# Single PSUM banks in the first token half of an MLP, its down pieces on two alternating pairs

## The chip, the cores and the metric

One core of one Trainium2 chip runs the kernel. The metric is the time of one execution in device microseconds. The kernel before takes 2958.96 us, the median of three runs (2958.73 to 2962.72). The profile is of one further execution.

The engines are named as the profile does: PE is TensorE (PEld its weight loads), DVE is VectorE, ACT is ScalarE, POOL is GpSimd, SP is SyncE, which here only issues DMAs. Each engine works through its instructions in the order in which the program issues them.

## The reference

```python
x = A_x                                            # [1, 2048, 576] float32
mod = (silu(c) @ w_mod).reshape(1, 6, 1, 576)
sa, ca, ga, sb, cb, gb = ...                       # six rows of 576
h = layernorm(x) * (1 + ca) + sa
q = h @ wq                                         # 32 heads of 128
k, v = the last 512 positions of the caches        # 16 heads, each for two q heads
o = softmax(q @ k^T * 128 ** -0.5) @ v
x = x + ga * (o @ wo)
h = layernorm(x) * (1 + cb) + sb
gate = h @ W_gate                                  # [2048, 4608]
up = h @ W_up
x = x + gb * ((relu(gate) * up) @ W_down)          # [4608, 576]
```

Everything is float32. The kernel keeps that precision by splitting an operand into a rounded part (hi) and the rest (lo): a product is three matmuls, hi by hi, hi by lo and lo by hi.

## The kernel before, in words

The program runs the attention first (128 units, one q head by 512 queries each) and the MLP after it. The 2048 rows of x lie in sixteen tiles acc0 to acc15 of 128 tokens by 576; attention and MLP both add their results into them.

**The MLP's passes.** The MLP works on one half of the tokens after the other (1024 tokens each). W_gate and W_up have 36 column tiles of 128 (NFT); a pass m takes two of them. NFP = 18 passes make a half, so m = 0 to 17 are the first half and m = 18 to 35 the second (NB = 36). The gate and up product of a pass is a 2 x 2 block product: two column tiles, two halves of the 576 inputs, two blocks of 512 tokens. It is done with seven products instead of eight (the scheme of Strassen and Winograd): P1, P6, P2, P7, P5, P4, P3, in this order (order). Each is a slot of the pass. A slot has two halves (prod), the gate's (xx = 0) and the up's (xx = 1), with seven matmuls of 512 columns each into one PSUM bank. P2 is accumulated onto P1's banks and P3 onto P5's, after those have been read.

**The extra operands.** The sums of weights that P6, P7, P5 and P3 need are made by VectorE from SBUF (w_sums, line 851: S1 in slot 1, S4 in slot 2, S3 and S2 of the next pass in slots 5 and 6) in the first half only. w_prep, two slots ahead of the product, splits them: ScalarE rounds (line 821) and GpSimd subtracts (lines 822 and 823). The split weights are also stored to DRAM, and the second half only loads them. From m = 5 on, the first half also prepares the second half's activations (h_later, lines 883 to 899, mostly GpSimd). Four times (m = 2, 4, 6, 8) half a block of second-half tokens is normalized (ln_half): VectorE's statistics, ScalarE's scaling, ten transposes by TensorE into PSUM in two steps (trans, line 1027), copies by ScalarE (line 1030) and stores to DRAM on SP's queue.

**After a product.** VectorE and ScalarE take the product out of PSUM (evac in the first half, evac_half in the second), combine it with the earlier ones, and form relu(gate) * up; ScalarE and GpSimd split the result (h_out, lines 1060 and 1061).

**The down product.** In the first half pass m - 1's down product runs in the slots of pass m, in eight pieces (md_piece, down_piece): a piece has twelve matmuls of 288 columns into a PSUM pair (two banks) and an addition into acc by VectorE (line 602). One piece lies between the two halves of every slot but the first, and one more stands at the end of slots 0 and 1. In the second half most passes (FAST, m = 18 to 33) do the down product with a scheme of seven products as well, in fourteen smaller pieces of six matmuls (fast_piece, line 671), run in the following pass. That scheme needs extra sums beside the result; they lie in acc0 to acc7, whose tokens are done. The first pass of it (FAST[0] = 18) writes them, by a copy on ScalarE (line 679); the later ones add (line 681).

**PSUM.** There are eight banks. In the first half of the MLP, three pairs rotate for gate and up: two of the pool psS (tag s) and one of psX (tag x); new_banks takes the next free one, and a pair goes back to the list free after its evacuation. The fourth pair, psW (tag w), takes every down piece. The transposes of ln_half take a pair of the rotation. In the second half psS is closed, and its four banks become psG: two tags, a and b, of two single banks each, so that the gate's bank and the up's bank are waited for apart; P1, P2, P5, P3 of an even pass use a and P6, P7, P4 use b, and the other way round in an odd one. Pair x is then free for the down pieces, which alternate between x and w (md_pool) from m = 19 on.

**Order of issue.** mlp_slots writes the order by hand. For a slot: the first half of the product, then sums and others (weight sums, splits, loads), then in the second half evac_half of the first bank, then a down piece with its addition, then the functions set by mat with sums=True, then the second half of the product, then the evacuation. The function mat(m, s, fn) places fn in slot s + 1 of pass m; with s = 5 it is P3's slot.

Of the kernel before, what the change touches and what calls it, by code (L numbers as in the profile page):

```python
# [7 lines left out]
F32 = mybir.dt.float32  # L8
# [6 lines left out]
P = 128  # L15
# [10 lines left out]
H2 = D // 2  # L26
# [5 lines left out]
def kernel(  # L32
# [13 lines left out]
    nc = tc.nc  # L46
# [594 lines left out]

    NFP = NFT // 2
    NB = 2 * NFP
    ds_, hhi, hlo = {}, {}, {}
    wop, wraw, hop = {}, {}, {}
    pair, tmp = {}, {}
# [13 lines left out]
    def fast_piece(m, kind, n):  # L660
        if kind == "4":
            specs = [(fop[m, "A22"], fw[m, "4"], 0, 2 * n + j) for j in range(2)]
        else:
            a, b = {"16": ("A11", "S2"), "75": ("S3", "S1"), "23": ("A12", "S4")}[kind]
            specs = [(fop[m, x], fw[m, kind], j * H2, n) for j, x in enumerate((a, b))]
        pool = md_pool()
        ps = pool[0].tile([P, 2, 512], F32, tag=pool[1], name=f"mf{m}_{kind}_{n}")
        for j, ((hi, lo), (whi, wlo), c, qt) in enumerate(specs):
            sl = slice(qt * P, (qt + 1) * P)
            for i, (x, w) in enumerate(((hi, whi), (hi, wlo), (lo, whi))):  # L670
                nc.tensor.matmul(ps[:, j, :H2], x[:, sl], w[:, c:c + H2], start=i == 0, stop=i == 2)  # L671
        if kind == "4":
            for j in range(2):
                a = acc[8 + 2 * n + j][:, :H2]
                nc.vector.tensor_tensor(a, ps[:, j, :H2], a, op=ALU.add)
            return
        a = acc[{"16": 0, "75": 4, "23": 12}[kind] + n].rearrange("p (h n) -> p h n", h=2)
        if kind != "23" and m == FAST[0]:
            nc.scalar.copy(a, ps[:, :, :H2])
        else:  # L680
            nc.vector.tensor_tensor(a, ps[:, :, :H2], a, op=ALU.add)

# [304 lines left out]
    def ln_half(qb, hh):  # L987

        ts = [4 * qb + 2 * hh, 4 * qb + 2 * hh + 1]
        st, xn = {}, []  # L990
        nm = f"lh{qb}_{hh}"
        cols = slice(256 * hh, 256 * hh + 256)

        def stats():
            mv = st["mv"] = sp.tile([P, 4, 2], F32, tag="mv", name=f"mv{nm}")
            for i, t in enumerate(ts):
                assert adds[t] == HQ // 2
                bn = sp.tile([P, 2, 6], F32, tag="st", name=f"st{nm}_{i}", bufs=1)
                for h in range(2):
                    nc.vector.bn_stats(bn[:, h, :], acc[t][:, h * H2:(h + 1) * H2])  # L1000
                nc.vector.bn_aggr(mv[:, i, :], bn)
            rs = st["rs"] = sp.tile([P, 2, 4], F32, tag="rs", name=f"rs{nm}")
            nc.gpsimd.tensor_scalar(rs[:, 0, :2], mv[:, :2, 1], EPS, None, op0=ALU.add)
            nc.gpsimd.tensor_tensor(rs[:, 0, :2], rs[:, 0, :2], mhalf[:, :2], op=ALU.pow)
            nc.gpsimd.tensor_tensor(rs[:, 1, :2], mv[:, :2, 0], rs[:, 0, :2], op=ALU.mult)
            nc.gpsimd.tensor_scalar(rs[:, 1, :2], rs[:, 1, :2], -1.0, None, op0=ALU.mult)

        def norm():
            for i, t in enumerate(ts):
                pool, tag = ((rp, "raw"), (xp, "xm"))[i]  # L1010
                n = pool.tile([P, 640], F32, tag=tag, name=f"xn{nm}_{i}")
                nc.scalar.activation(n[:, :D], acc[t], AF.Identity, bias=st["rs"][:, 1, i:i + 1],
                                     scale=st["rs"][:, 0, i:i + 1])
                xn.append(n)

        def trans(ds):
            ps, k = new_banks(f"lt{nm}_{ds[0]}")
            free.append(k)
            ps = ps.rearrange("p a (b n) -> p (a b) n", b=2)
            p = 64 if ds[0] == 4 else P  # L1020
            if ds[0] == 4:
                f = hp.tile([P, 512], F32, tag="hT", name=f"lf{nm}_4").rearrange("p (a n) -> p a n", a=2)
            else:
                f = wp.tile([P, 4, 256], F32, tag="wC", name=f"lf{nm}_0")
            for j, d in enumerate(ds):
                for i in range(2):
                    nc.tensor.transpose(ps[:p, j, i * P:(i + 1) * P], xn[i][:, d * P:d * P + p], ident)
            add, mul = mods["b"]
            for j, d in enumerate(ds):
                nc.scalar.activation(f[:p, j, :], ps[:p, j, :], AF.Identity, bias=add[:p, d:d + 1],  # L1030
                                     scale=mul[:p, d:d + 1])
                hb_store(qb, d, cols, f[:p, j, :])

        return [stats, norm, lambda: trans((4,)), lambda: trans((0, 1, 2, 3))]

    def prod(m, s, n, xx):

        hs, w = hop[m // NFP, OPS[s][1]], wop[n]
        ps = pair[m, s][:, xx, :] if m < NFP else pair[m, s][xx]
        ops = []  # L1040
        for t in range(2):
            ops += [(w[:, xx, t, :], hs[t]), (w[:, xx, 3 + t, :], hs[t]), (w[:, xx, t, :], hs[3 + t])]
        ops.append((w[0:96, xx, 2, :], hs[2][0:96]))
        for i, (a, c) in enumerate(ops):
            nc.tensor.matmul(ps, a, c, start=s not in ("P2", "P3") and i == 0, stop=i == len(ops) - 1,  # L1045
                             skip_group_check=True)
# [101 lines left out]
    def md_pool():  # L1148
        px["n"] = px.get("n", 0) + 1
        return (px["x"], "x") if px["n"] % 2 else (psW, "w")  # L1150

    def new_banks(nm):
        npair[0] += 1
        k = free.pop(0)
        return (px["x"] if k == "x" else psS).tile([P, 2, 512], F32, tag=k, name=nm), k

    def new_pair(m, s):
        if m < NFP:
            pair[m, s], kind[m, s] = new_banks(f"gu{npair[0]}")
            return  # L1160
        if "g" not in px:
            open_g()
        kind[m, s] = "ab"[(s in ("P6", "P7", "P4")) ^ m % 2]
        pair[m, s] = [px["g"].tile([P, 512], F32, tag=kind[m, s], name=f"gh{m}_{s}_{i}") for i in range(2)]
# [220 lines left out]
    def mat(m, s, fn, sums=False):  # L1385
        mextra.setdefault((m, s, sums) if s < 6 else (m + 1, -1, sums), []).append(fn)

    for m in range(NB):
# [3 lines left out]
        for f in range(2):  # L1392
            for k, fn in enumerate(wd_prep(m, f)):
                if m >= NFP:
                    at_ = m, 3 + f
# [5 lines left out]
    fast_end()  # L1401
    for i in range(4):
        m = 2 + 2 * i
        for at_, fn in zip(((m - 1, 5), (m, 2), (m, 3), (m, 4)), ln_half(2 + i // 2, i % 2)):
            mat(*at_, fn, sums=at_ == (m - 1, 5))
    later = {s: [fn for t in range(3) for fn in h_later(1, s, t)] for s in TERMS}
    for i, fn in enumerate(later.pop("B11") + later.pop("B21")):
        mat(5 + i // 3, (0, 2, 4)[i % 3], fn)
# [18 lines left out]

    def mlp_slots():
        for m in range(NB):
            md = [lambda k=k, qt=qt: md_piece(m - 1, k, qt, md_pool() if m > NFP else None)  # L1430
                  for k in range(2) for qt in range(4)] if m else []
            if m - 1 in FAST:
                md = fast_pieces(m - 1)
            for i, s in enumerate(order(m)):
                flush_stores()
                if s not in ("P2", "P3"):
                    new_pair(m, s)
                else:
                    pair[m, s], kind[m, s] = (x[m, {"P2": "P1", "P3": "P5"}[s]] for x in (pair, kind))
                prod(m, s, 7 * m + i, 0)  # L1440
                if m or i:
                    sums(m, i)
                    others(m, i)
                if m >= NFP:
                    evac_half(m, s, 0)
                if m and i or m - 1 in FAST:
                    md.pop(0)()
                elif filler and not m:
                    filler.pop(0)()
                for fn in mextra.pop((m, i - 1, True), []):  # L1450
                    fn()
                prod(m, s, 7 * m + i, 1)
                wop.pop(7 * m + i)
                if m >= NFP:
                    evac_half(m, s, 1)
                if m and i < 2 or m - 1 in FAST:
                    md.pop(0)()
                elif filler and not i:
                    filler.pop(0)()
                if m < NFP:  # L1460
                    evac(m, s)
                if s not in ("P1", "P5") and m < NFP:
                    free.append(kind[m, s])
                yield
        for k in range(2):
            for qt in range(4):
                md_piece(NB - 1, k, qt, md_pool())
        flush_stores()
        assert not mextra and not filler
# [203 lines left out]
```

## Time and profile before

| | before |
|---|---|
| median of three runs | 2958.96 us |
| the profiled execution | 2957.22 us |
| its span | 2955.4 us |
| TensorE busy | 2871.7 us, 97% |
| VectorE busy | 2184.3 us, 74% |
| ScalarE busy | 1434.2 us, 49% |
| GpSimd busy | 2196.4 us, 74% |
| mean granted clock of TensorE | 0.991 |
| first token half of the MLP | about 1652 to 2322 us |

The times of the trace count from the start of the span. In the list of waits a row names who waited and for whom, then microseconds in total, times, and the longest. In the chain of waits a row is a start, a duration and a piece of work; x12 is one down piece, x7 one half of a product. In the timeline a bracket at the end of a row is the idle time before it and who ended it. A row by stretches has its length and then each engine's busy time with the number of instructions, the granted clock, the DMA engines' share and GB/s.

### The profile page before, as it was taken

The numbers are of one execution on the slowest core, as the hardware profiler recorded it, in microseconds if no ns is written. First come the engines' busy times: TensorE is split into PE (matmuls) and PEld (weight loads), VectorE is DVE, ScalarE is ACT, GpSimd is POOL, SyncE is SP. The second block draws the span as 40 slices with busy tenths as digits, with TensorE's granted clock in tenths as the row PEclk, the third lists the DMA queues.
The fourth block names the chain that finished last, engine by engine and source line by source line (L and its number), as shares of the span: only waits on it lengthen the run. The fifth ranks groups of instructions, "written<-read, shape, count | busy, mean of one in ns | idle before, by whom it ended". The sixth has DMA issues, their size and how long they took to land.

```text
span 2955.4 us, 41574 instructions
## 1 busy us (share of the span) xinstructions
PE 2871.7 (97%) x15256; PEld 2496.5 (84%) x15256; DVE 2184.3 (74%) x3058; ACT 1434.2 (49%) x2015; POOL 2196.4 (74%) x1597
## 2 busy tenths in 40 slices
PE   6889999999999999999999999999999999999999
PEld 5678888888888888888888788888888888888888
DVE  5778888788788888777889677777777556666665
ACT  3656666666676666666656433333323132222220
POOL 3767888788888889877778666667777477777773
PEclk8999999999999999999999999999999999999999
DMA  5312222222223223322144355566667944444443
GB/s 182 118 68 87 85 86 83 70 100 85 94 84 112 84 69 122 110 69 85 65 144 139 111 195 206 211 224 237 240 225 247 328 142 150 161 156 150 151 150 136
DMA packets 165899, 410.61 MB, mean 139 GB/s; under 512 B 15040, under 2 KB 61888, under 8 KB 165696
## 3 DMA queue, kind: packets, MB, share of 16 engines
q1 hardware_dynamic: 132944, 289.23, 30.3%
q10 hardware_dynamic: 32752, 118.73, 10.1%
q8 instruction: 121, 1.98, 0.3%
q14 instruction: 82, 0.67, 0.1%
HBM read 275.81 MB, written 160.40 MB: 148 GB/s over the span
## 4 chain that ended last, share of the span: by engine, by line
PE 85%; DVE 6%; POOL 3%; ACT 2%; DMA 2%; issue 2%; SPq 0%; ACTq 0%; DVEq 0%; POOLq 0%
PE gh_P L1045 13%; PE wo L591 13%; PE qps L388 12%; PE gu L1045 11%; PE md L591 8%; PE mf L671 6%; PE s L464 3%; PE s L463 3%; PE s L462 3%; PE pv L566 3%; PE pv L565 3%; PE pv L564 3%; DVE wr L851 2%; POOL lo L546 1%; PE qm L490 1%
## 5 line engine op out<-in xcount | busy, mean ns | idle before, releaser
L546 POOL TENSOR_TENSOR lo<-p,hi 128x1024 fp32r<-128x1024 f32 x256 | 611.7, 2411 | 0.0
L555 POOL TENSOR_TENSOR ks<-ks,p 128x512 f32<-128x512 f32 x256 | 344.1, 1344 | 284.1 <-ACT p L539 213.5
L467 DVE TRANSPOSE_TENSOR_REDUCE t<-s 128x32 f32<-128x1024 f32 x256 | 316.3, 1243 | 136.5 <-PE s L464 125.5
L537 DVE TENSOR_TENSOR p<-s,mb 128x1024 f32<-128x1024 f32 x250 | 295.2, 1219 | 4.2
L388 PE MATMUL qps<-hTa,wA 128*128 128x512 f32 x1176 | 285.4, 393 | 4.4 <-ACT wA L186 2.0
L591 PE MATMUL wo<-woga,ohi 128*128 128x288 f32 x1344 | 279.9, 301 | 0.0
L591 PE MATMUL md<-wogb,hhi 128*128 128x288 f32 x1280 | 263.1, 298 | 14.6 <-DVE acc L602 14.6
L539 ACT ACTIVATE p<-p 128x1024 f32<-128x1024 f32 x250 | 264.1, 1056 | 17.6 <-DVE p L537 15.7
L526 ACT CAST hi<-p 128x1024 fp32r<-128x1024 f32 x256 | 269.0, 1051 | 7.0
L388 PEld LDWEIGHTS qps<-hTa,wA 128*128 128x128 f32 x1176 | 223.0, 190 | 53.3 <-ACT wA L186 2.7
L1045 PE MATMUL gh_P<-hop_T,wop 128*128 128x512 f32 (+1 forms) x1008 | 255.8, 393 | 1.3 <-DMA wop<-wk_P 1.3
L442 ACT ACTIVATE qhi<-qps 128x512 fp32r<-128x512 f32 x128 | 76.5, 597 | 341.6 <-PE qps L388 341.6
L591 PEld LDWEIGHTS md<-wogb,hhi 128*128 128x128 f32 x1280 | 214.2, 189 | 29.5 <-DVE acc L602 18.6
L602 DVE TENSOR_TENSOR acc<-md,acc 128x576 f32<-128x576 f32 x160 | 120.8, 755 | 147.8 <-PE md L591 146.9
L591 PEld LDWEIGHTS wo<-woga,ohi 128*128 128x128 f32 x1344 | 218.4, 189 | 6.6
L1045 PEld LDWEIGHTS gh_P<-hop_T,wop 128*128 128x128 f32 (+1 forms) x1008 | 181.4, 188 | 33.2 <-DMA wop<-wk_P 1.7
L591 PE MATMUL wo<-woga,olo 128*128 128x288 f32 x672 | 198.5, 295 | 0.4 <-POOL olo L580 0.2
L1045 PE MATMUL gh_P<-hop_B,wop 128*128 128x512 f32 (+1 forms) x756 | 192.7, 395 | 0.0
L591 PE MATMUL md<-wogb,hlo 128*128 128x288 f32 x640 | 189.9, 297 | 0.0
L1045 PE MATMUL gu<-hop_B,wop 128*128 128x512 f32 (+1 forms) x756 | 187.4, 394 | 0.0
L600 ACT COPY acc<-wo 128x576 f32<-128x576 f32 x232 | 147.7, 636 | 69.2 <-PE wo L591 61.7
L580 POOL TENSOR_TENSOR olo<-rb,ohi 128x512 fp32r<-128x512 f32 x128 | 167.1, 1305 | 16.8 <-ACT ohi L576 16.5
(275 smaller groups left out, 7651.3 us busy)
## 6 DMA issues: line engine op xcount, KB each, us to landing
wop<-wk_P SPq DMA_DIRECT2D x133, 640.0 KB
wk_P<-wop ACTq DMA_DIRECT2D x119, 640.0 KB
wr<-wlay SPq DMA_DIRECT2D x68, 384.0 KB
againq<-akq SPq DMA_DIRECT2D x22, 640.0 KB
againo<-ako SPq DMA_DIRECT2D x18, 576.0 KB
rogb<-wd SPq DMA_DIRECT2D x36, 288.0 KB
rwA<-wq SPq DMA_DIRECT2D x32, 320.0 KB
wlay<-wg SPq DMA_DIRECT2D x36, 256.0 KB
```

Of the source, the lines that this page charges most:

```text
L388: return [lambda i=i, a=a, b=b: nc.tensor.matmul(ps, a, b, start=(i == 0), stop=(i == n - 1)) for i, (a, b) in enumerate(ops)]
L467: nc.vector.tensor_reduce(t4[u][:, 2 * h:2 * h + 2, :].rearrange("p k b -> p (k b)"), t.rearrange("p k (b j) -> p (k b) j", j=32), axis=AX ...
L526: nc.scalar.copy(hi_[u, h], pt[u, h])
L537: nc.vector.tensor_tensor(p, t, bc[u][:, None, :].to_broadcast([P, 2, 512]), op=ALU.subtract)
L539: nc.scalar.activation(p, p, AF.Exp, bias=0.0, scale=1.0)
L546: nc.gpsimd.tensor_sub(lo_[u, h], pt[u, h], hi_[u, h].bitcast(F32))
L555: nc.gpsimd.tensor_tensor(ks_[u], ks_[u], p[:, j, :], op=ALU.add)
L580: nc.gpsimd.tensor_sub(olo[u], o.pop(u), ohi[u].bitcast(F32))
L591: nc.tensor.matmul(ps[:, half, :H2], a[:, sl], w[b][:, cs], start=(n == 0 and seed is None), stop=(n == 5), skip_group_check=seed is not None)
L600: nc.scalar.copy(av, ps[:, :, :H2])
L671: nc.tensor.matmul(ps[:, j, :H2], x[:, sl], w[:, c:c + H2], start=i == 0, stop=i == 2)
L1045: nc.tensor.matmul(ps, a, c, start=s not in ("P2", "P3") and i == 0, stop=i == len(ops) - 1, skip_group_check=True)
```

## The change

A constant NG = 1 takes the place of NFP wherever the choice between pairs and single banks is made. So only pass 0 still rotates three pairs; from m = 1 on gate and up use the single banks of psG and evac_half. All down pieces of m = 1 on alternate between x and w. The transposes of ln_half take a turn in that alternation, and the step with four blocks moves from slot 5 of its pass, ahead of the down piece, to slot 6, behind it. The first extra sums of the second half are copied by VectorE instead of ScalarE.

```diff
+    NG = 1
...
         if kind != "23" and m == FAST[0]:
-            nc.scalar.copy(a, ps[:, :, :H2])
+            nc.vector.tensor_copy(a, ps[:, :, :H2])
...
         def trans(ds):
-            ps, k = new_banks(f"lt{nm}_{ds[0]}")
-            free.append(k)
+            pool = md_pool()
+            ps = pool[0].tile([P, 2, 512], F32, tag=pool[1], name=f"lt{nm}_{ds[0]}")
...
-        ps = pair[m, s][:, xx, :] if m < NFP else pair[m, s][xx]
+        ps = pair[m, s][:, xx, :] if m < NG else pair[m, s][xx]
...
     def new_pair(m, s):
-        if m < NFP:
+        if m < NG:
...
-        for at_, fn in zip(((m - 1, 5), (m, 2), (m, 3), (m, 4)), ln_half(2 + i // 2, i % 2)):
-            mat(*at_, fn, sums=at_ == (m - 1, 5))
+        for at_, fn in zip(((m - 1, 5), (m, 2), (m, 3), (m, 5)), ln_half(2 + i // 2, i % 2)):
+            mat(*at_, fn, sums=at_[1] == 5)
...
-            md = [lambda k=k, qt=qt: md_piece(m - 1, k, qt, md_pool() if m > NFP else None)
+            md = [lambda k=k, qt=qt: md_piece(m - 1, k, qt, md_pool())
...
-                if m >= NFP:
+                if m >= NG:
                     evac_half(m, s, 0)
...
-                if m >= NFP:
+                if m >= NG:
                     evac_half(m, s, 1)
...
-                if m < NFP:
+                if m < NG:
                     evac(m, s)
-                if s not in ("P1", "P5") and m < NFP:
+                if s not in ("P1", "P5") and m < NG:
                     free.append(kind[m, s])
```

## The prediction

> **What bounds the kernel now.** I read the page's first lines, then the list of waits of TensorE from 1640 us on, then busy time per loop pass in the MLP's first token half, then the chain of waits inside it.
>
> ```profile
> span 2955.4 us, 41574 instructions
> PE 2871.7 (97%) x15256; PEld 2496.5 (84%) x15256; DVE 2184.3 (74%) x3058; ACT 1434.2 (49%) x2015; POOL 2196.4 (74%) x1597
> ```
>
> ```profile
> PE md L591 <- DVE acc L602: 14.6, 9, 3.6
> PE mf L671 <- ACT acc L679: 2.3, 1, 2.3
> PE gh_P L1045 <- DMA wop<-wk_P: 1.3, 1, 1.3
> ```
>
> TensorE is the bound; only what it idles, or does slowly, can be won. The largest wait is that of a down piece (md) for VectorE's add of the piece before it, since all of them use one PSUM pair (w). The passes m = 1 to 16, cut at the start of P3's up half (time, PE, PEld, DVE, ACT, POOL, granted clock, DMA share, GB/s):
>
> ```profile
> 1693.29:1728.57 35.28, 35.28 (x195) 31.23 (x195) 24.83 (x28) 10.93 (x17) 22.13 (x21) 1.00 0.57 202
> 1728.57:1764.99 36.42, 36.42 (x205) 32.18 (x205) 28.77 (x33) 14.60 (x23) 23.51 (x25) 1.00 0.56 199
> ...
> 2021.66:2059.31 37.65, 35.55 (x196) 31.14 (x195) 28.05 (x28) 12.09 (x17) 30.93 (x26) 1.00 0.64 230
> 2059.31:2094.63 35.32, 35.32 (x196) 31.14 (x195) 25.37 (x28) 12.03 (x17) 28.23 (x24) 1.00 0.71 257
> ...
> sum 590.19, PE 575.54 PEld 505.29 DVE 434.75 ACT 200.40 POOL 422.91; mean PE 44.27 PEld 38.87 DVE 33.44 ACT 15.42 POOL 32.53
> ```
>
> An undisturbed pass takes 35.28 us, one with a norm half (m = 2, 4, 6, 8) 36.42. Sixteen of them would be 16 x 35.28 + 4 x 1.14 = 569.0; they took 590.2. Of the 21.2 above that, 590.19 - 575.54 = 14.6 are idle; the rest is work at a lower clock. The chain shows where:
>
> ```profile
> 2130.66 3.11 PE md L591 x12
> 2133.77 5.12 PE gu L1045 x21
> ...
> 2169.43 1.86 PE md L591 x12
> 2171.29 4.83 PE gu L1045 x21
> 2176.12 1.60 PE md L591 x12
> ...
> 2196.95 1.62 PE gu L1045 x7
> ...
> 2200.65 7.22 DVE wr L851
> ...
> 2208.59 2.63 PE md L591 x12
> 2211.23 5.62 PE gu L1045 x21
> ```
>
> ```profile
> 2130.66 0.71 PE L591 MATMUL md<-wogb,hhi 128*128 128x288 f32 x2 [2.35 <-DVE acc L602]
> ```
>
> A piece that follows a stall costs 1.85 to 3.11 instead of 1.60: 1.51 + 0.29 at 2130, 1.03 + 0.79 at 2208, 0.25 at each of the other seven, 5.4 together (1.2 of the 21.2 I leave unexplained and don't count). The late adds stand behind the weight sum S3 (wr L851), whose length isn't its own:
>
> ```profile
> L851 DVE TENSOR_TENSOR wr<-wr,wr x17: 948/1736/7219, 1687.4 to 2277.6; 128x768 f32<-128x768 f32 x17
> ```
>
> ```profile
> 2205.80 1.25 POOL L895 TENSOR_TENSOR hx_T<-hx_T,hy_T 128x512 fp32r<-128x512 f32 x1
> 2211.32 1.28 POOL L1061 TENSOR_TENSOR hlo<-r,hhi 128x512 fp32r<-128x512 f32 x1 [4.27 <-ACT hhi L1060]
> ```
>
> Alone it takes 0.95; at 2200.65 it ended 0.82 after GpSimd's run of work did (2207.05). GpSimd then idled 4.27 until VectorE's next result: a lock lasts until GpSimd has nothing left that doesn't need VectorE.
>
> **The change part by part.** (1) Down pieces alternate between w and x. A piece in slots 2 to 6 now has its buffer back if the add of the piece two before is done: 8.0 us or more after that one's end instead of 3.2 (a slot is 1.60 + 1.60 + 1.60 = 4.8); around P1 and P6 4.8 instead of 1.6. The longest stall, 3.6, is under the 4.8 that is gained. Removed: 14.6 + 5.4 = 20.0 us.
>
> (2) The price: gate/up has two pairs, of four single banks, instead of three pairs in rotation. P1 of the next pass takes P4's banks. With P4's slot starting at T, P1's gate half wants its bank at T + 9.6 and its up half at T + 11.2 (P1's halves follow each other). VectorE's order is now S3, P4's first op, md add, P4's two last ops. Durations:
>
> ```profile
> L1174 DVE TENSOR_TENSOR q<-gu,q x18: 1208/1214/1224, 1665.0 to 2297.0; 128x1024 f32<-128x1024 f32 x18
> L1170 ACT COPY q<-gu x18: 1011/1017/1018, 1658.6 to 2289.5; 128x1024 f32<-128x1024 f32 x18
> ```
>
> ```profile
> L602 DVE TENSOR_TENSOR acc<-md,acc 128x576 f32<-128x576 f32 x50 | 37.8, 755 | 44.9 <-PE md L591 44.9
> L1111 DVE TENSOR_TENSOR q<-gh_P,q 128x512 f32<-128x512 f32 x36 | 24.9, 692 | 34.6 <-PE gh_P L1045 32.4 <-ACT q L1105 2.2
> L1105 ACT COPY q<-gh_P 128x512 f32<-128x512 f32 x36 | 20.9, 587 | 43.2 <-PE gh_P L1045 43.2
> ```
>
> S3 at the worst ended at 2207.87, with T = 2198.57 (end of the 1.62 at 2196.95): T + 9.3. Then P4's first op ends at T + 10.0 (0.4 late), the add at 10.7, the last two at 12.1 (some 0.5 later still): 1.0 us of stall where 3.6 were. A more usual lock:
>
> ```profile
> 1866.04 5.72 DVE L851 TENSOR_TENSOR wr<-wr,wr 128x768 f32<-128x768 f32 x1
> ...
> 1868.59 1.77 PE L1045 MATMUL gu<-hop_B,wop 128*128 128x512 f32 x7
> ...
> 1872.48 0.53 PE L591 MATMUL md<-wogb,hhi 128*128 128x288 f32 x2 [2.12 <-DVE acc L602]
> ```
>
> P3's start at 1868.59 puts T at 1863.8 and the end of S3 at T + 7.9: 8.6, 9.4 and 10.7 for the three, all in time, nothing left. Halving the evacuations adds 2 x 0.692 - 1.214 for P6 and the same for P7 (same shape), 0.34 us of VectorE a pass, and 2 x 0.587 - 1.017 = 0.16 of ScalarE; both have idle time for it (24.8 and 10.9 busy of 35.28), and the first op of P5, P4 and P3 now runs under the down piece, so results are out 0.7 earlier. If that cover is gone (VectorE behind after a lock), the 0.34 is paid, 6 us over 17 passes.
>
> (3) The norm half's transposes leave the gate/up pairs for the alternating ones, the four-block one a slot later.
>
> ```profile
> ACT lflh L1030 <- PE md L591: 9.9, 2, 5.0
> ```
>
> ScalarE's copies waited for a wC buffer that the last down piece frees, up to 5.0; behind that piece the wait is gone. Their four stores on SP's queue move behind a load of the next pass's raw weights and one of down weights. Who reads them is h_later's loads, the nearest two slots on (m = 9, slot 1), so I cost that at nothing; were those late, GpSimd would wait in its queue ahead of a weight split, up to a slot of 4.8, once or twice. New is that the transposes want their pair at T + 8.0, against the add at 9.4 of a 5.72 lock: 1.4 us in each of m = 6 and 8, where GpSimd's h_later work has begun; 2.7 together. Bounds: 0 (no lock there) to 5.
>
> (4) The switch to the single banks comes at m = 1, not 18. By the rotation P3 sits at both places in the second of the two s pairs, and at 18 the switch cost no wait:
>
> ```profile
> 2320.20 3.39 PE L1045 MATMUL gh_P<-hop_B,wop 128*128 128x512 f32 x14
> ```
>
> So 0; if P1 were put on P3's banks, three ops of 0.69: 2.1.
>
> (5) The first extra sums, eight pieces in m = 19:
>
> ```profile
> 2371.34 1.17 ACT L679 COPY acc<-mf 128x576 f32<-128x576 f32 x2
> ```
>
> ```profile
> 2372.02 1.06 PE mf L671 x6
> 2373.08 2.80 PE gh_P L1045 x7
> 2375.88 1.18 PE mf L671 x6
> ...
> 2378.68 0.80 PE mf L671 x6
> ```
>
> ```profile
> L681 DVE TENSOR_TENSOR acc<-mf,acc x40: 746/757/758, 2389.2 to 2498.4; 128x576 f32<-128x576 f32 x40
> ```
>
> ScalarE got to its copies only behind casts that waited for GpSimd; TensorE lost the 2.3 and then 0.26 + 1.20 + 0.38 at a low clock: 4.2. VectorE's copy is not in this trace; the add of the same shape is its upper bound (0.757; the lower is ScalarE's 0.59), and from m = 20 on it does twelve such adds a pass with TensorE never idle:
>
> ```profile
> 2400.00:2900.00 500.00, 500.00 (x2693) 437.51 (x2692) 308.17 (x458) 116.65 (x205) 358.90 (x302) 1.00 0.47 156
> ```
>
> So all 4.2 are won. That row also shows two gate/up pairs and two down pairs sufficing, without S sums on VectorE.
>
> Sum: 20.0 + 4.2 - 1.0 - 2.7 = 20.5. The profiled execution took 2957.2 (span 2955.4 and 1.8 around it), 1.7 below the median of the three runs: 2957.2 - 20.5 + 1.7 = 2938.4.
>
> The Trainium skill (TensorE: Matmul & The Clock Gate, Part 1: The HAM clock gate) has the clock fall after an idle window of about 3.4 us; here pieces went to nearly double after gaps of 2.3 and 2.35, so the trace disagrees. By the page only the 3.6 gap would have cost clock, and the sum would be some 5 us smaller.
>
> **The rivals.** Half the gain: locks get longer as passes get denser. GpSimd's 30.93 of 37.65 us at m = 9 become 88% of 35.28. Each microsecond by which S3 ends beyond T + 8.4 is paid by P1's up half (S3's end + 0.69 + 0.76 + 1.39 against 11.2). If it ends 1 us later than now in the thirteen passes from m = 5, they lose about 0.5 to 1 each, 10 in all: 2948. For it: density. Against: m = 10 ran undisturbed with 28.23 of GpSimd in 35.32.
>
> Slower: the same place with locks that end 2.5 us later (T + 10.4 for the usual one). P1 then waits 2.0 in thirteen passes, 26, and at gaps of that size the clock falls too, 0.25 to 1.5 each, say 10: 24.2 won, 36 lost, 2971. It decides from 24.2 / 13 = 1.9 us a pass, S3 ending at T + 10.3 on average; the worst seen is 9.3, once, and GpSimd's 4.27 idle shows the lock ending for lack of work. The Trainium skill (SBUF — State Buffer, SBUF: two separate sides) says of the port that VectorE and GpSimd share that the loser fully blocks; the 7.22 beside 0.95 agrees, and the rule sets no limit to such a lock.
>
> Nothing in the first half (a wait of another engine takes each place), only the 4.2: 2954.7. Against it: the list of waits names no other wait over 1.3 in TensorE's MLP time.
>
> **How the numbers follow.** Forecast 0.60, half gain 0.20, nothing but the extra sums 0.08, slower 0.12. A measurement of this kernel tells a change from none at about 0.2%, 5.9 us. So faster 0.80, same 0.08, slower 0.12. The range starts at 2931 (no stall left, the unexplained 1.2 won too: 2957.2 - 25.4 + 1.7 = 2933.5, and 2 for what the runs vary) and ends at 2954, which takes in half the gain and most of nothing.
>
> **What would show it.** TensorE's wait for acc L602 should fall from 14.6 to under 2, ACT acc L679 vanish; passes of 35.3 from m = 5 on; waits of gh_P or lt for VectorE of some 4 us in all. Wrong if gh_P waits for P4's ops in most passes, or if S3's longest grow past 9 us.

## The result, and the profile after

| | before | after |
|---|---|---|
| median | 2960.84 us (4 runs) | 2932.98 us (4 runs) |
| ratio | | 0.9905, 95% interval 0.9888 to 0.9922 |
| the profiled execution, span | 2957.22 us, 2955.4 us | 2930.96 us, 2929.2 us |

The change makes the kernel about 28 us faster. The page and TensorE's waits from 1640 us on, of the changed kernel (line numbers are one higher than before from line 644 on):

```profile
span 2929.2 us, 41722 instructions
PE 2862.0 (98%) x15256; PEld 2492.8 (85%) x15256; DVE 2198.4 (75%) x3100; ACT 1431.8 (49%) x2024; POOL 2195.3 (75%) x1597
```

```profile
PE mf L672 <- POOL fp_S L699: 0.9, 1, 0.9
PE gh_P L1046 <- DMA wop<-wk_P: 0.9, 1, 0.9
```

These are the only waits of TensorE left that belong to the MLP. The 14.6 us for acc L602 and the 2.3 us for ScalarE's acc are gone. TensorE's busy time fell by 9.7 us (2871.7 to 2862.0) with the same 15256 matmuls: 8.1 from P3's up half in pass 0 on, the work at a lower clock, and 1.6 ahead of it, where the change alters nothing. By stretches, one pass and then the sixteen passes:

```profile
2155.62:2190.90 35.28, 35.28 (x196) 31.23 (x195) 27.30 (x28) 12.22 (x18) 30.37 (x26) 1.00 0.68 245
...
1692.53:2261.83 569.30, 569.30 (x3145) 503.73 (x3145) 444.63 (x489) 202.21 (x306) 423.13 (x379) 1.00 0.64 232
```

Sixteen passes take 569.3 us, where the undisturbed passes of before add up to 569.0. One with 30.37 us of GpSimd in 35.28 is as even as the rest.

The locks on S3 did not go. Its lengths (least, median, longest, in ns) in the changed kernel:

```profile
L852 DVE TENSOR_TENSOR wr<-wr,wr x17: 951/4252/5646, 1686.7 to 2255.2; 128x768 f32<-128x768 f32 x17
```

The median rose from 1736 to 4252 ns. The longest of them, in the timeline of VectorE and in the chain of waits:

```profile
2184.25 5.65 DVE L852 TENSOR_TENSOR wr<-wr,wr 128x768 f32<-128x768 f32 x1
2189.82 0.68 DVE L1079 TENSOR_TENSOR r<-gh_P,r 128x512 f32<-128x512 f32 x1
2190.42 0.74 DVE L602 TENSOR_TENSOR acc<-md,acc 128x576 f32<-128x576 f32 x1
2191.09 0.68 DVE L1082 TENSOR_TENSOR gh_P<-gh_P,r 128x512 f32<-128x512 f32 x1
2191.80 0.69 DVE L1083 SCALAR_TENSOR_TENSOR r<-r,gh_P 128x512 f32<-128x512 f32 x1
```

```profile
2181.28 3.22 PE gh_P L1046 x14
2184.49 1.60 PE md L591 x12
2186.09 3.22 PE gh_P L1046 x14
2189.30 1.60 PE md L591 x12
2190.90 4.83 PE gh_P L1046 x21
```

The 14 halves-of-a-product matmuls at 2181.28 are P5's up half and P4's gate half, so P4 starts at T = 2182.9. S3 ends at 2189.9, T + 7.0. P4's first op is done at 2190.5, and P1's gate half, the second third of the x21, starts at 2192.5. P4's last op is done at 2192.5, and P1's up half, the last third, starts at 2194.1. TensorE goes through without a gap, 2.0 and 1.6 us clear.

### The profile page after: what moved, and what is told of

Read it like the earlier page. It is cut to its first block, busy times and chain, and to the rows that moved or that the text cites. A ratio compares the mean times of both kernels' runs of the same rounds, so it can differ in the third digit from the quotient of the medians.

```text
span 2929.2 us, 41722 instructions
## 1 busy us (share of the span) xinstructions
PE 2862.0 (98%) x15256; PEld 2492.8 (85%) x15256; DVE 2198.4 (75%) x3100; ACT 1431.8 (49%) x2024; POOL 2195.3 (75%) x1597
## 3 DMA queue, kind: packets, MB, share of 16 engines
q10 hardware_dynamic: 32752, 118.73, 10.3%
## 4 chain that ended last, share of the span: by engine, by line
PE 89%; DVE 3%; POOL 3%; ACT 2%; DMA 2%; issue 2%; SPq 0%; POOLq 0%; ACTq 0%; DVEq 0%
PE gh_P L1046 26%; PE wo L591 13%; PE qps L388 12%; PE md L591 8%; PE mf L672 6%; PE s L464 4%; PE s L463 4%; PE s L462 3%; PE pv L566 3%; PE pv L565 3%; PE pv L564 3%; POOL lo L546 1%; PE qm L490 1%; DVE t L467 1%; ACT p L539 1%
## 5 line engine op out<-in xcount | busy, mean ns | idle before, releaser
L1046 PE MATMUL gh_P<-hop_B,wop 128*128 128x512 f32 (+1 forms) x1470 | 366.9, 393 | 0.0
L1046 PE MATMUL gh_P<-hop_T,wop 128*128 128x512 f32 (+1 forms) x1246 | 315.9, 393 | 0.9 <-DMA wop<-wk_P 0.9
L1046 PEld LDWEIGHTS gh_P<-hop_B,wop 128*128 128x128 f32 (+1 forms) x1470 | 267.7, 188 | 49.1
L1046 PEld LDWEIGHTS gh_P<-hop_T,wop 128*128 128x128 f32 (+1 forms) x1246 | 225.3, 188 | 41.2 <-DMA wop<-wk_P 1.3
L602 DVE TENSOR_TENSOR acc<-md,acc 128x576 f32<-128x576 f32 x160 | 120.6, 754 | 107.2 <-PE md L591 107.1
```

## The experiments

Times are ratios to runs of the kernel before that were timed beside each, with a 95% interval; one percent is 29.6 us.

**1. The alternation without the single banks.** Whole pairs stay, two of them (tag s) rotate, and x goes to the down pieces.

```diff
-    NG = 1
+    NG = NFP
...
-        free.append("x")
```

> Change without the single banks: gate and up of the first half keep whole pairs, now two that rotate (x goes to the down pieces), evacuated after both halves; down pieces and transposes alternate between x and w, and VectorE copies the first extra sums. My theory: the wait of md for acc L602 goes, but P1 of the next pass now needs all of P4's evacuation, which ends 0.75 + 2.08 us after S3 on VectorE and is wanted 9.6 us after P4's start; locks as in the kernel before (S3 ending at 8.0 in five passes, 8.2 and 9.5 in two) then cost 1.2 to 2.7 each, 6 to 10 us in all with the lower clock: 18 to 22 us faster than before, not 27. Rival (the down pair was all of it, single banks give nothing): 27 us faster, no wait of gu for VectorE.

Measured: 2942.45 us, ratio 0.9933 (0.9917 to 0.9950), 20 us faster than before. Its waits:

```profile
PE gu L1046 <- DVE r L1071: 8.5, 6, 3.0
PE gh_P L1046 <- DVE q L1071: 2.2, 1, 2.2
PE gu L1046 <- DVE q L1071: 1.1, 2, 0.6
```

No down piece waits any more, and P1 waits for the whole pair's last op instead. One of the three rows is the switch to single banks at pass 18, where with two pairs P3 did sit on the banks that P1 takes. The rival that the down pair was all of it falls.

**2. The single banks without the alternation.** All down pieces of the first half stay on w, and the transposes take x.

```diff
-md_piece(m - 1, k, qt, md_pool())
+md_piece(m - 1, k, qt, md_pool() if m > NFP else None)
...
-            pool = md_pool()
+            pool = px["x"], "x"
```

> Change without the alternation: gate and up on single banks from pass 1 on, but every down piece of the first half on pair w again; transposes take x; VectorE copies the first extra sums. My theory: the piece in P3's slot wants the add of P4's piece 6.4 us after P4's start, and that add now stands behind S3 and P4's first op; with S3 ending at 5 to 7.2 as in the changed kernel, twelve passes lose about 0.5 to 2 us, 12 to 16 in all plus some 5 of lower clock: 5 to 12 us faster than before, with md waiting for acc L602 some 12 to 16 us. Rival (the earlier, halved evacuation is what frees TensorE): 25 us faster.

Measured: 2950.27 us, ratio 0.9962 (0.9949 to 0.9976), 11 us faster. From its waits and from its page:

```profile
PE md L591 <- DVE acc L602: 16.1, 13, 3.3
```

```profile
PE 2864.1 (97%) x15256; PEld 2489.8 (84%) x15256; DVE 2198.1 (75%) x3100; ACT 1430.8 (49%) x2024; POOL 2188.3 (74%) x1597
```

The wait for the add is as long as before, in more and shorter pieces. TensorE's busy time is 2864.1, beside 2872.0 in experiment 3, which has the old banks and the same extra sums. Cut into what lies ahead of P3's up half in pass 0 and the first half from there to the same place in pass 17 (experiment 2, then 3):

```profile
0.00:1689.92 1689.92, 1627.70 (x8516) 1405.16 (x8516) 1351.62 (x2023) 1082.91 (x1465) 1326.75 (x839) 0.99 0.29 97
1689.92:2315.86 625.94, 609.81 (x3340) 534.83 (x3339) 467.17 (x517) 211.86 (x321) 436.45 (x397) 1.00 0.65 229
```

```profile
0.00:1693.05 1693.05, 1630.44 (x8515) 1407.90 (x8516) 1352.40 (x2023) 1082.87 (x1465) 1326.63 (x839) 0.99 0.29 97
1693.05:2324.05 631.00, 614.69 (x3340) 538.81 (x3339) 464.89 (x482) 209.94 (x304) 441.40 (x397) 0.99 0.64 227
```

Of the 7.9 us, 2.7 lie ahead of the first half, where the two do the same work, and 4.9 in it. But in the kernel before, with the old banks too, the first half took 625.3 us with 610.7 busy, as much as here: single executions of the same first half differ by 5.7 us. So the medians (2950.27, and 2958.93 in experiment 3) put some 9 us on the single banks, and the profiles don't show where they are won.

**3 and 4. The first extra sums, done alone and undone.**

```diff
# 3: the kernel before with
-            nc.scalar.copy(a, ps[:, :, :H2])
+            nc.vector.tensor_copy(a, ps[:, :, :H2])
# 4: the changed kernel with the reverse
```

> The kernel before with one part of the change alone: VectorE copies the first extra sums. My theory: TensorE's wait for acc L679 (2.3 us) and the 1.8 us at a lower clock behind it go: 4.2 us faster, the first half as before (md waits 14.6 us). Rival (the next wait takes its place, or VectorE is late): 0 to 1 us.

> The changed kernel with that one part undone: ScalarE copies the first extra sums. My theory: 4.2 us slower than the changed kernel, so 23 to 24 us faster than before, and TensorE waits 2.3 us for ScalarE's acc in pass 19. Rival: no difference to the changed kernel, 27 to 28 us faster than before.

Measured: alone 2958.93 us, ratio 0.9989 (0.9980 to 0.9998), 3.3 us faster; undone 2937.24 us, ratio 0.9919 (0.9903 to 0.9935), against 0.9905 of the changed kernel, 4 us slower than it. Both are near the 4.2 that was reckoned, though the second rests on two intervals that overlap. In the profile it is clear, since the wait for ScalarE's copy is absent from the one and back in the other:

```profile
PE mf L672 <- ACT acc L680: 2.3, 1, 2.3
PE gh_P L1046 <- DVE r L1079: 2.2, 1, 2.2
...
PE gh_P L1046 <- POOL wop L824: 1.2, 1, 1.2
```

The two rows on gh_P are of another kind: in this execution of experiment 4, one S3 was held up for 9.85 us (timelines of VectorE, GpSimd and TensorE):

```profile
2187.52 9.85 DVE L852 TENSOR_TENSOR wr<-wr,wr 128x768 f32<-128x768 f32 x1
2197.29 0.68 DVE L1079 TENSOR_TENSOR r<-gh_P,r 128x512 f32<-128x512 f32 x1
```

```profile
2195.29 1.26 POOL L896 TENSOR_TENSOR hx_T<-hx_T,hy_T 128x512 fp32r<-128x512 f32 x1
2200.69 1.30 POOL L1062 TENSOR_TENSOR hlo<-r,hhi 128x512 fp32r<-128x512 f32 x1 [4.14 <-ACT hhi L1061]
```

```profile
2198.11 3.81 PE L1046 MATMUL gh_P<-hop_B,wop 128*128 128x512 f32 x14 [2.23 <-DVE r L1079]
```

S3 ended 0.8 us after GpSimd ran out of work (2196.55), and P1's gate half waited 2.23 us for P4's first op. It ended at T + 11.2 (T = 2186.15), and the first half of this execution took 608.7 us instead of the 604.6 of the changed kernel. This is the place at which the prediction put the price of the change, and a lock over 9 us was one of its signs of being wrong. A long lock pays the price; the two profiled executions of the changed kernel itself had none as long.

**5, 6 and 7. A delay behind S3.** Eight (5, 6) or fourteen (7) statistics ops of VectorE behind each S3; a row of experiment 6 has 136 of them at 440 ns, and eight take some 2.9 us from start to start.

```diff
         nc.vector.tensor_tensor(flat(out), flat(a), flat(b), op=op)
+        if s == "S3":
+            late_ = sp.tile([P, 2, 6], F32, tag="st", name=f"wait{m}", bufs=1)
+            for i in range(8):                       # 14 in experiment 7
+                nc.vector.bn_stats(late_[:, i % 2, :], acc[12][:, :H2])
```

> The kernel before with eight extra statistics ops on VectorE (about 0.41 us each, 3.3 in all, results unused) right behind every S3. My theory: a piece stalls by what S3 with its delay ends later than 5.85 us after P4's start; with the ends of the kernel before plus 3.3 the wait for acc L602 grows from 14.6 to about 40 us, and with the lower clock behind it the kernel is 30 to 40 us slower than before. Rival (VectorE has idle time in each pass, 35.3 less some 27 us busy, and takes it in): 0 to 5 us.

> The changed kernel with the same eight ops (3.3 us) behind every S3. My theory: P1 of the next pass stalls by what S3 with its delay ends later than about 8.6 us after P4's start; the changed kernel's ends (4.8 to 7.2 in the passes from 5 on) plus 3.3 give 0 to 1.9 us a pass, 11 us in all, now as a wait of gh_P for VectorE, and some 2 us of lower clock: 11 to 14 us slower than the changed kernel. Rival (slack is larger, VectorE's idle time takes it): 0. Rival (no slack left): 3.3 us in each of 16 passes, 50.

> The changed kernel with fourteen such ops (5.7 us) behind every S3. My theory: by the same sum 1.9 to 4.3 us in each of the twelve passes from 5 on, 39 us in all, none in passes 1 to 4 (ends at 2.5 plus 5.7), and 5 to 12 us of lower clock: 44 to 51 us slower than the changed kernel, slower than the kernel before too. Rival (slack is larger by a slot): under 10.

Measured: experiment 5, on the kernel before, 3000.4 us, ratio 1.0129 (1.0100 to 1.0159), 38 us slower, as expected. On the changed kernel experiment 6 gave 2957.38 us, ratio 0.9990 (0.9978 to 1.0002), 24 to 25 us slower than the changed kernel where 11 to 14 were expected; experiment 7 gave 2984.79 us, ratio 1.0077 (1.0047 to 1.0106), 51 to 52 us slower where 44 to 51 were. From the waits of 5, of 6 and of 7 (in 6 and 7 line numbers are four higher, so r L1083 is P4's first op):

```profile
PE md L591 <- DVE acc L602: 38.1, 17, 5.0
```

```profile
PE gh_P L1050 <- DVE r L1083: 5.7, 5, 2.6
PE ltlh L1032 <- DVE acc L602: 4.3, 2, 2.2
PE gh_P L1050 <- POOL wop L824: 2.9, 5, 1.2
PE gh_P L1050 <- DMA wop<-wk_P: 2.5, 1, 2.5
```

```profile
PE gh_P L1050 <- DVE r L1083: 22.7, 9, 3.9
PE ltlh L1032 <- DVE acc L602: 10.0, 4, 4.3
```

So both deadlines of the prediction are real: P1's gate half waits for P4's first op, and the transposes for their pair, 5.7 + 4.3 = 10.0 us beside the 11 expected. Two things were missing from the expectation. A late S3 makes S2 late too, and with it a weight split (wop L824, 2.9). And the low clock behind the stalls was far underrated: TensorE's busy time on the page of experiment 6 is 2871.3,

```profile
PE 2871.3 (97%) x15256; PEld 2494.8 (84%) x15256; DVE 2246.0 (76%) x3236; ACT 1432.3 (48%) x2024; POOL 2198.7 (74%) x1597
```

9.3 us over the changed kernel's, for 14.5 us of added waits (the four rows above, less the 0.9 for the DMA that the changed kernel has too). In the changed kernel the longest lock left 2.0 and 1.6 us to spare at P1's two halves; 2.9 us of delay is past that margin, and 20 us and more are lost.

**8. The kernel before without GpSimd's part of h_later.**

```diff
         def comb(i):
-            x, y = st["a"][:n], st["b"][:n]
-            nc.gpsimd.tensor_tensor(x, x, y, op=...)
...
-                nc.gpsimd.tensor_sub(lo, a, hi.bitcast(F32))
+                nc.scalar.copy(lo[:, 0:16], a[:, 0:16])
...
-                nc.gpsimd.tensor_sub(hi[64:96], a[64:96], hi[64:96].bitcast(F32))
```

> The kernel before without GpSimd's part of h_later (its sums and remainders of the second half's activations are left out, so the second half's gate and up are computed from incomplete operands; loads, casts and stores stay). My theory: S3 is long only because GpSimd's work holds it up; without that work S3 takes 1 to 2 us, ends at 2.5 to 4 us after P4's start in every pass, and the wait for acc L602 falls from 14.6 to under 2 us: 16 to 21 us faster than before, on one down pair. Rival (one pair is too few by itself): the wait stays over 8 us.

Measured: 2940.57 us, ratio 0.9927 (0.9899 to 0.9956), 22 us faster, on one down pair and with three gate/up pairs; in the profiled execution the first half is 15.6 us shorter (609.7 for 625.3). S3's lengths in it, and its wait for the add:

```profile
L851 DVE TENSOR_TENSOR wr<-wr,wr x17: 951/951/5207, 1684.1 to 2258.5; 128x768 f32<-128x768 f32 x17
```

```profile
PE md L591 <- DVE acc L602: 3.5, 3, 1.6
```

S3's median falls to its own length, and three stalls of nine are left, 3.5 us instead of 14.6 (under 2 were expected). So GpSimd's work did make the stalls, through the length of S3; not all of it was h_later's, since three passes still had locks of 4.5 to 5.2 us.

**9 and 11. S3 issued behind the down piece, and the changed kernel beside it.**

```diff
-        for k, s in {1: [(0, "S1")], 2: [(0, "S4")], 5: [(1, "S3")], 6: [(1, "S2")]}.get(i, []):
+        for k, s in {1: [(0, "S1")], 2: [(0, "S4")], 6: [(1, "S2")]}.get(i, []):
...                                                   # in mlp_slots, behind the first md.pop(0)()
+                if i == 5 and 0 < m + 1 < NFP:
+                    w_sums(m + 1, "S3")
```

> The changed kernel with S3 issued behind the down piece of P4's slot instead of ahead of P4's first op: only P4's last two ops are left behind it before P1 needs the bank. My theory: S3 starts some 2.5 us later and, as its lock lasts until GpSimd is out of work, ends at most 1 to 2 us later (6 to 9 us after P4's start); P1's up half allows 9.8 now. The changed kernel has no such wait in its profile, so it gains only where an execution has a long lock: 0 to 2 us faster than the changed kernel beside it. Rival (the lock lasts a fixed time from S3's start): ends at 7.3 to 9.7, and the weight split of P6 that needs S2 behind it becomes late: 3 to 10 us slower than the changed kernel.

> The changed kernel itself, on the chip and against the runs of the kernel before that the last one is timed with: 25 to 29 us faster than before. In its profile my theory expects S3 held up in every pass from 5 on, as in the first profile, and a wait of gh_P for VectorE only where S3 ends more than 8.6 us after P4's start.

Measured: 2933.11 us, ratio 0.9904 (0.9887 to 0.9920), and the changed kernel 2933.34 us, ratio 0.9902 (0.9888 to 0.9917). There is no difference. S3 in pass 5, first in the changed kernel and then in experiment 9:

```profile
1864.51 5.18 DVE L852 TENSOR_TENSOR wr<-wr,wr 128x768 f32<-128x768 f32 x1
```

```profile
1865.35 2.65 DVE L852 TENSOR_TENSOR wr<-wr,wr 128x768 f32<-128x768 f32 x1
```

P4's slot starts at 1862.97 and 1861.28 in them, so S3 starts at T + 1.5 and T + 4.1 and ends at T + 6.7 in both: a lock has no fixed length. What ended it shows in GpSimd's timelines of the two:

```profile
1868.14 0.73 POOL L823 TENSOR_TENSOR wop<-wr,wop 32x256 fp32r<-32x256 f32 x1
1868.84 1.99 POOL L824 TENSOR_TENSOR wop<-wr,wop 128x512 fp32r<-128x512 f32 x1
```

```profile
1866.44 0.73 POOL L823 TENSOR_TENSOR wop<-wr,wop 32x256 fp32r<-32x256 f32 x1
1867.14 2.00 POOL L824 TENSOR_TENSOR wop<-wr,wop 128x512 fp32r<-128x512 f32 x1
```

GpSimd was not out of work. S3 ended 0.8 us behind the small subtraction of a weight split (L823, done at 1868.87 and 1867.17), while the large one (L824) followed at once and took 2.0 us instead of 1.3. In all these traces an S3 of over 2 us ends 0.82 to 0.88 us behind the end of some GpSimd operation. Of the twelve in the first profile of the changed kernel, nine end behind L823 in this way, and only three where GpSimd had no next operation ready. The 9.85 us of experiment 4 lasted over such a place, so why VectorE gets in there in one pass and not in another stays open. Nor is the end the same in every pass: in pass 7 it is T + 6.7 and, issued later, T + 8.1, in pass 10 T + 6.5 and T + 10.3.

The later S3 wins nothing. The changed kernel had no wait there that could go, and S2 behind S3 now makes a weight split late (the waits of experiment 9; in the profiled execution its first half takes 607.7 us against 604.6):

```profile
PE gh_P L1046 <- POOL wop L824: 1.8, 4, 0.6
```

Experiment 11 is a second profile of the changed kernel. Again gh_P never waits for VectorE. From P3's up half in pass 0 to the end it takes 1236.8 us, as the first one does, 25.5 less than before. S3 was held up in ten of the twelve passes from 5 on, not in every one as expected: in passes 7 and 12 it took its own 0.95.

Not tried is the change without moving the transposes to slot 6. By the order of issue the program would stand still: their copies wait for a buffer that the last down piece of the pass frees, and with the alternation that piece waits for the pair that these copies free.

## Why the prediction was right, point by point

The forecast was 2938 us with 20.5 us won; the median moved by 27.9, and the profiled execution by 26.3 (2957.2 to 2930.96). Direction, range and the places of gain and price held; two terms were mis-sized, and what ends a lock was described wrongly.

**The bound.** Right. The first half's stretch, from P3's up half in pass 0 to that in pass 17, went from 625.3 us (1693.29 to 2318.60) to 604.6 (1692.53 to 2297.10): 20.7 of the 26.2 by which the span fell. From there to the end 4.7 are won, and 0.8 lies ahead of the first stretch, which the change doesn't touch; that stretch ahead varied from 1689.8 to 1695.6 us over the profiled executions of this case.

**Term 1, the down pieces, 20.0 us.** Right, and slightly small: the 1.2 us that the prediction left unexplained were won too. They were busy time as well, since TensorE's in sixteen passes fell from 575.5 to 569.3, within 0.3 us of the undisturbed sum.

**Term 2, P1 on P4's banks, minus 1.0 us.** Mis-sized: 0 in both profiled executions of the changed kernel. The place is right (P1 waits for P4's first op in experiments 4, 6 and 7), but the prediction took the one lock of 7.22 us over from the trace of before. S3 now starts some 0.75 us earlier, and none of its seventeen lasted over 5.65, ending at T + 7 at the latest. Experiment 4, whose first half is the same program, had 9.85 us once and lost 4.1 in this half. So the price is paid in some executions and not in others, and that the profiled one paid nothing is partly luck.

**What ends a lock.** Wrong. The prediction let a lock last until GpSimd has nothing left that doesn't need VectorE. That holds for the 7.22 us that it showed and for three of the twelve in the changed kernel; the other nine end behind the small subtraction of a weight split, with GpSimd's next operation at hand (experiment 9). This subtraction is now done earlier: in pass 5 at T + 5.9, where it was T + 7.1 before (1870.94), and S3 ends at T + 6.7 instead of T + 8.0. The sum doesn't rest on this rule, since terms 2 and 3 took the ends of S3 over from the trace of before; but these ends moved with GpSimd's weight split, and so both terms came out too large.

**Term 3, the transposes, minus 2.7 us.** Mis-sized: 0. The prediction put a lock of 5.72 us into passes 6 and 8, taken from pass 5. In pass 6 there was one, but of 4.25 us (timelines of VectorE and TensorE in the changed kernel; pass 8 has the same):

```profile
1900.02 4.25 DVE L852 TENSOR_TENSOR wr<-wr,wr 128x768 f32<-128x768 f32 x1
...
1904.80 0.74 DVE L602 TENSOR_TENSOR acc<-md,acc 128x576 f32<-128x576 f32 x1
```

```profile
1906.51 1.04 PE L1028 MATMUL ltlh<-ident,xnlh 128*128 128x128 f32 x8
```

The add that the transposes need was done 1.0 us ahead of them. In experiment 6, 2.9 us later, exactly these two passes stalled, 2.2 us at most each.

**Term 5, the extra sums, 4.2 us.** Right: 3.3 done alone, 4 undone, and 4.7 from pass 18 to the end, in which the wait for a DMA fell from 1.3 to 0.9 as well.

**The rest.** The switch at pass 1 cost nothing, as reckoned. VectorE's busy time rose by 14.1 us (2184.3 to 2198.4): 9.1 in the first half (457.5 to 466.6), for the halved evacuations and longer holds of the weight sums, and 5.2 behind it, where the eight copies of the extra sums take 6.0. All of it is covered.

**The rivals.** Half the gain, through longer locks: they did become more frequent, twelve S3s over 2 us where there were eight, but not longer, and its threshold of T + 8.4 was not reached in the changed kernel's profiles (experiment 4 reached it once). The slower one needed S3 to end at T + 10.3 on average; experiment 7, with some 5 us behind an S3 that ends at T + 5 to 8, puts it past there and is slower than the kernel before by 0.8%. So the rival's place was right, and its condition did not come about. Both rivals count thirteen passes from m = 5 on; S3 is made for the next pass, so there are twelve. Nothing in the first half: excluded.

**The clock rule.** The Trainium skill (TensorE: Matmul & The Clock Gate, Part 1: The HAM clock gate) with its idle window of about 3.4 us would, by the prediction's estimate, have made the gain some 5 us smaller. The trace disagrees further than the prediction said: from P3's up half in pass 0 on 8.1 us of busy time vanished together with stalls of which only one was over 3.4 us.

## What to carry to other kernels

When one engine's queue holds an operation that another engine can hold up, look at which buffer is wanted soonest behind it, and spread the buffers so that each is wanted some microseconds later than the longest hold-up ends. Here neither half of the trade was enough: of 28 us, the second down pair with whole gate/up pairs won 20, the single banks with one down pair 11 (each with the 3 to 4 of the extra sums in it, and the second not traced to a place). Cost a stall of TensorE with the slower matmuls behind it, which here added a third to six tenths of the stall's own length.

## What the runs showed that was not expected

A stall costs more than its idle time, but not at a fixed rate. In the changed kernel the first half is busy for 604.6 us and never idle. Beyond that, the profiled executions had in this half:

| | idle, us | more busy, us |
|---|---|---|
| before | 14.6 | 6.1 |
| experiment 3 | 16.3 | 10.1 |
| experiment 2 | 16.1 | 5.2 |
| experiment 6 | 13.6 | 8.0 |
| experiment 7 | 33.8 | 17.8 |
| experiment 5 | 38.2 | 20.9 |

That is 0.3 to 0.6 us for each one idle. Why some gaps of 2.1 us are followed by slow matmuls at once and others not was not settled.

VectorE's hold-up by GpSimd reached 9.85 us for an operation of 0.95. It always ended 0.8 to 0.9 us behind the end of a GpSimd operation, mostly not behind the last one at hand.
